# Eight tiles of P in the ring of attention, and low-half P V products one block later

## The chip, the cores and the metric

The kernel runs on one core of one Trainium2 chip. The metric is the device time of one execution in microseconds. Three runs of the kernel before took 2016.7, 2019.44 and 2020.83 us, so the median is 2019.44 us. The core has five engines that run their own instruction queues in order and wait for each other by semaphores: TensorE (PE in the profile, with weight loads apart as PEld), VectorE (DVE), ScalarE (ACT), GpSimd (POOL) and SyncE (SP, which here issues DMAs).

## The reference

A block of a transformer with adaptive layer norms: multi-head attention, then a token-shifting mixer and an MLP. What the change touches is the attention, and at its end the tiles of the tails. Cut to that:

```python
B, S, D, H = 1, 2048, 512, 32          # 32 heads of 16
mod = (_silu(c) @ w_mod).reshape(c.shape[0], 6, 1, -1)   # sa, ca, ga, sb, cb, gb
h = _layernorm(x) * (1 + ca) + sa
q, k, v = split(h @ wqkv)
scores = jnp.einsum("bhqd,bhkd->bhqk", q, k) * (Dh ** -0.5)
p = _softmax(scores, axis=-1)
o = jnp.einsum("bhqk,bhkd->bhqd", p, v)
x = x + ga * (o @ wo)
h = _layernorm(x) * (1 + cb) + sb
x = x + gb * _B_ref(h, w1, w2, w3, w4)  # layernorm, gelu, shifts by 1 and 2 tokens, MLP
```

All inputs are float32. The kernel keeps that precision by splitting operands into a high and a low half and adding up the products.

## The kernel before, in words

Attention is cut into 64 **units**. A unit is one quarter of the queries (512 of 2048) for one pair of heads, and has 16 **steps**, one for each 128 keys. There are 1024 steps, 256 for each quarter of the queries. A quarter of the queries is followed by a **tail** (output projection, second layer norm, mixer, MLP); three of the tails run after attention, and the first one starts 30 steps before its end.

For a step s and each of its two heads j the engines do this:

- PE computes scores into one PSUM bank (`sc`, L1012), ACT takes their exponential into the tile `pt[s]` (`pt<-sc`, L1008). `pt[s]` holds 2 x 512 words of 32 bits; the upper 16 bits of a word are read as float16, the high half of P.
- PE also computes the scores of step s+24 into another bank (`mb`, L996), and DVE reduces them to their maximum (`mx`, L992), which is needed when that unit begins. Four bank fills a step, two for ACT and two for DVE, share 7 PSUM banks (`NSM`).
- `p_low` (L1050) turns the lower 16 bits of `pt[s]` in place into a float16 number, the low half of P: one instruction of 128x1024 on POOL (L1061), or the same on ACT (L156 in the profile, a helper's line). The planner takes ACT when POOL's planned start is over 200 ns behind ACT's.
- PE multiplies V with P into the unit's own bank `pv`: four products of the high half for each step (L1086), and four of the low half for each pair of steps (L1083). "High product" and "low product" below mean such a group of four.

When a unit's last products are in, ACT copies `pv` to SBUF (`ac`, L1103), and only then may the first high product of the next unit start, as there is one `pv` bank. PE then transposes `ac` in four products (`ot`, L1113; eight records in the trace), ACT copies them (`sm`, L1120), DVE takes a reciprocal (`rc`, L1128), and POOL scales the result (`osb`, L1124). A unit's maxima are finished by one instruction on DVE (`mf`, L1042), two on ACT (`mf`, `nm`, L1043 and L1044) and one on POOL (`nm`, L1045).

The order of each engine's instructions is written out by the program. A planner (`Sched`) keeps one estimated clock for each engine. The loop at L1621 walks over **blocks** of three half steps (a half step is one head of one step). In each block it puts on PE a **row** (three `sc` and three `mb`), then the low halves that are due (on POOL or ACT), and then a **column**, the high and low products of what was computed two blocks earlier (`LAG`). Before a block, the planned clock of PE is set forward to when the banks of the row and the P of the column are ready, and if that leaves a gap of 500 ns, waiting work, such as `ot`, is put there. So the planned times decide which engine gets a low half and where `ot` and other small work stands; how long anything takes on the chip they don't decide.

The ring of P has six tiles (`NPT`). A tile comes free when PE has done the low product that reads it. A pair's low product stands two blocks behind its scores, and the next scores into the same tile come later on PE than it.

`fa` is a pool of SBUF that is opened after the first quarter of attention, when what held the weights of Q, K and V is closed. It holds the tiles of the tails, among them `xb` (4 of 128x512, float32) and `xn` and `xf` (3 each). The tails use them only from the last 30 steps on.

Of the kernel before, what the change touches and what calls it, by code (L numbers as in the profile page):

```python
# [8 lines left out]
F32 = mybir.dt.float32  # L9
# [3 lines left out]
I32 = mybir.dt.int32  # L13
# [7 lines left out]
S, D, H, DH, F = 2048, 512, 32, 16, 1792  # L21
P = 128
KT = D // P
NKT = S // P
CH = 512
# [58 lines left out]
XBF = 4  # L84
XBT = 4
# [7 lines left out]
XN = {"xn": 3, "xf": 3, "x4": 2}  # L93
# [5 lines left out]
NPT = 6  # L99
# [6 lines left out]
LNG = (1, 3)  # L106
LNC = 2
VP = 2
XB = 4


# [219 lines left out]
def kernel(ctx, tc, A_x, A_wqkv, A_wo, B_w1, B_w2, B_w3, B_w4, c, w_mod, out):  # L331
# [58 lines left out]
    for j in range(2):  # L390
        x = [ident[:, 64 * j + VD * a:64 * j + VD * a + DH + 1] for a in range(3)]
# [343 lines left out]
    for i in range(NV):  # L735
        t = qp.tile([P, H // 4, 192], BF16, name=f"vt{i}")
# [234 lines left out]
        sch.dma(dma.dma_start, vst[u], Vs[units[u][1]])  # L971

    sm = Slots(NSM)
    e_exp, e_hi, e_low, v_free, acs = {}, {}, {}, [0.0], []

    def bank(nm):
# [3 lines left out]
    def max_part(m, j):  # L980
# [14 lines left out]
                max_fin(u)  # L995
        return ready, lambda: te.matmul(b, lhs, kst[u % 3][r, c * CH:(c + 1) * CH], start=True, stop=True), after  # L996

    def score_part(s, j):

        u, kt = divmod(s, NKT)  # L1000
        if j == 0:
            pt[s] = at.tile([P, 2, CH], I32, name="pt", tag="pt", bufs=NPT)
        x, b = bank("sc")
        ready, sm.t[x] = sm.t[x], LATE
        r = slice(64 * j, 64 * j + 64)

        def after(e):
            ea = sch.crit("A", 480, e + PX, lambda: act.activation(pt[s][:, j], b, AF.Exp))  # L1008
            sm.t[x] = ea + XP["A"]
            if j:  # L1010
                e_exp[s] = e_hi[s] = ea
        return ready, lambda: te.matmul(b, kst[u % 3][r, kt * P:(kt + 1) * P], qst[u][r], start=True, stop=True), after  # L1012
# [210 lines left out]
    def pool_of(ci):  # L1223
        return fa if ci < NB or (ci - NB) % 2 else tp
# [58 lines left out]
    def tail(ci):  # L1283
# [91 lines left out]
        def normed(key, t, rs):  # L1375
            tag = xtag(key, t)
            xlive[tag] = xlive.get(tag, 0) + 1
            x = xn[key, t] = (tp if tag == "x4" else fa).tile([P, D], F32, name="xn", tag=tag, bufs=XN[tag])
            y = xbt[t]
            return ln_apply(x, y, rs), mark((key, t))  # L1380

# [15 lines left out]
        for i, t in enumerate(new):  # L1397
# [2 lines left out]
            yield from wo_mm(i, range(KT))  # L1400
            b = banks.pop(i)
            x1 = x1t[t]
            xb = xbt[t] = pool_of(ci).tile([P, D], F32, name="xb", tag="xb", bufs=XBF if pool_of(ci) is fa else XBT)

            def x1_add(x1=x1, b=b):
                dve.tensor_tensor(x1, x1, b, op=OP.add)
# [190 lines left out]


    blocks = [list(range(i, min(i + GRP, 2 * NS))) for i in range(-2 * LEAD, 2 * NS, GRP)]
    pvs = [x for s in range(0, NS, 2) for x in ((s, 0), (s + 1, 0), (s, 1))]  # L1600
    due = 0.0
    for k, blk in enumerate(blocks + [[]] * (LAG + CPER)):
        if blk and blk[0] <= LENDS <= blk[-1]:
# [69 lines left out]
        if blk and blk[0] <= 2 * (NS - T0L) <= blk[-1]:  # L1673
            sch.add(tail_loads())
# [56 lines left out]
```

## Time and profile before

| | us |
|---|---|
| median of the runs | 2019.44 |
| span of the profiled execution | 2019.7 |
| start, projections and the first quarter of attention, up to about step 264 | 550 |
| steps after the first quarter, looked at from 575 to 1480 | 905 |
| end of attention with the start of the first tail, 1480 to 1540 | 60 |
| tails, 1540 to the end | 480 |

The profile is of one execution. Its span, from the first instruction to the last, is 2019.7 us, which lies within the three runs, 0.3 us above their median; no time of its own is given for what lies around the span. The views used below are: busy time by stretch of time; groups of instructions, with the idle time of their engine ahead of them; who waited for whom; and the order of time of one engine, where neighbours of one kind are merged into one row (`x6` is six of them, the number behind the start is from the first's start to the last's end, and square brackets give idle time ahead and who ended it). Starts are counted from the span's start.

### The profile page before, as it was taken

Reading aid. Unit: us, or ns where it says so; the run is one execution under the profiler, and the core shown is the slowest. Engines: PE = TensorE matmul, PEld = TensorE weight load, DVE = VectorE, ACT = ScalarE, POOL = GpSimd, SP = SyncE. Lnnn points to the kernel's source line nnn. Section 1 sums busy time; section 2 is a strip of 40 time slices with the busy share of each in tenths; the row PEclk is TensorE's granted clock in tenths of the full one; section 3 lists DMA queues with packets and bytes.
Section 4 is the critical chain, followed back from the end, with each engine's and each line's share of the span. In section 5 each row is a group of like instructions: output and inputs, shape, how many; then the busy total and the mean of one; then the engine's idle time right before and its main releaser. Section 6 shows DMA issues by size and latency. Waiting matters only on the chain.

```text
span 2019.7 us, 41655 instructions
## 1 busy us (share of the span) xinstructions
PE 1934.4 (96%) x14456; PEld 1162.1 (58%) x14456; DVE 1656.3 (82%) x2979; ACT 1510.2 (75%) x3085; POOL 1571.9 (78%) x1488
## 2 busy tenths in 40 slices
PE   7999999999999999999999999999998999999999
PEld 5755545454444444444444444444455878898998
DVE  6398888879999999999999999999975886556443
ACT  6438987768999999999999999999985544344443
POOL 6349988879999999999999999999996554435222
PEclk9989999999999999999999999999999999999999
DMA  8777675445343434444443435354414676553541
GB/s 295 233 204 192 151 187 155 135 130 124 86 92 87 91 88 83 96 82 97 81 98 75 104 72 107 72 136 126 99 46 158 230 261 265 226 200 116 201 153 68
DMA packets 185508, 278.01 MB, mean 138 GB/s; under 512 B 117104, under 2 KB 127856, under 8 KB 169008
## 3 DMA queue, kind: packets, MB, share of 16 engines
q1 hardware_dynamic: 181792, 267.20, 49.1%
q10 hardware_dynamic: 2304, 4.20, 0.6%
q0 software_dynamic: 1200, 3.93, 0.5%
q8 instruction: 115, 1.88, 0.4%
q14 instruction: 97, 0.79, 0.1%
HBM read 211.81 MB, written 62.91 MB: 136 GB/s over the span
## 4 chain that ended last, share of the span: by engine, by line
PE 61%; DVE 16%; ACT 9%; issue 6%; POOL 4%; DMA 3%; SPq 0%; ACTq 0%; POOLq 0%; DVEq 0%
PE mb L996 13%; DVE mx L992 12%; PE pv L1086 9%; PE sc L1012 8%; ACT pt L1008 7%; PE w L363 5%; PE w L359 5%; PE w L361 5%; PE pv L1083 4%; PE ot L1113 3%; POOL pt L1061 2%; PE xT L1247 1%; POOL trs L1356 1%; PE v L359 1%; DMA wr<-Ws 1%
## 5 line engine op out<-in xcount | busy, mean ns | idle before, releaser
L1061 POOL TENSOR_SCALAR pt<-pt 128x1024 f16<-128x1024 uint16 x953 | 1248.3, 1367 | 79.9 <-ACT pt L1008 76.7
L992 DVE TENSOR_REDUCE mx<-mb 128x1 f32<-128x512 f32 x2048 | 1250.0, 681 | 72.7 <-PE mb L996 63.5
L1008 ACT ACTIVATE pt<-sc 128x512 int32<-128x512 f32 x2048 | 1060.9, 614 | 123.5 <-PE mb L996 97.1
L996 PE MATMUL mb<-kst,qtl 62*128 62x512 f32 x2048 | 781.1, 461 | 20.5 <-ACT pt L1008 10.0
L1012 PE MATMUL sc<-qtl,kst 64*128 64x512 f32 x2048 | 739.3, 449 | 4.6 <-DVE mx L992 1.8
L996 PEld LDWEIGHTS mb<-kst,qtl 62*128 62x128 f32 x2048 | 358.9, 193 | 233.7 <-ACT pt L1008 160.4
L1012 PEld LDWEIGHTS sc<-qtl,kst 64*128 64x128 f32 x2048 | 336.6, 185 | 185.4 <-DVE mx L992 118.7
L1086 PE MATMUL pv<-pt,vst 128*32 128x512 f16 x4096 | 384.8, 397 | 20.6 <-ACT ac L1103 20.6
L1460 POOL TENSOR_TENSOR g<-sq,g 128x256 fp32r<-128x256 f32 (+1 forms) x124 | 96.8, 785 | 188.9 <-ACT g L1459 176.6
L1083 PE MATMUL pv<-pt,vst 128*32 128x512 f16 (+1 forms) x2048 | 220.8, 389 | 2.5 <-POOL pt L1061 2.4
L1086 PEld LDWEIGHTS <-vst 128*32 128x32 bf16 x4096 | 91.8, 93 | 227.2 <-issue 208.8
L361 PE MATMUL w<-A,wr 128*128 128x256 f32 (+1 forms) x520 | 153.4, 295 | 0.3 <-DVE A L349 0.3
L359 PE MATMUL w<-A,wr 128*128 128x256 f32 (+1 forms) x520 | 153.2, 295 | 0.3 <-ACT A L353 0.3
L363 PE MATMUL w<-A,wr 128*128 128x256 f32 (+1 forms) x520 | 153.1, 294 | 0.0
L1456 ACT ACTIVATE sq<-w 128x256 f32<-128x256 f32 (+1 forms) x130 | 52.1, 401 | 127.0 <-PE w L363 117.5
L363 PE MATMUL w<-wr,g 128*128 128x512 f32 x270 | 106.5, 394 | 3.1 <-POOL g L1460 3.1
L359 PE MATMUL w<-wr,g 128*128 128x512 f32 x270 | 106.9, 396 | 1.8 <-DMA wr<-Ws 1.8
L361 PE MATMUL w<-wr,g 128*128 128x512 f32 x270 | 106.1, 393 | 0.0
L1438 DVE SCALAR_TENSOR_TENSOR sq<-sq,w 128x256 f32<-128x256 f32 (+1 forms) x130 | 58.1, 449 | 56.5 <-ACT sq L1458 56.3
L359 PEld LDWEIGHTS w<-A,wr 128*128 128x128 f32 x520 | 98.7, 190 | 1.7 <-ACT A L353 0.5
L361 PEld LDWEIGHTS w<-A,wr 128*128 128x128 f32 x520 | 98.7, 190 | 1.6 <-DVE A L349 0.5
L363 PEld LDWEIGHTS w<-A,wr 128*128 128x128 f32 x520 | 98.6, 190 | 0.5 <-issue 0.5
(156 smaller groups left out, 2131.6 us busy)
## 6 DMA issues: line engine op xcount, KB each, us to landing
wr<-Ws SPq DMA_DIRECT2D x66, 1024.0 KB, 5.2
vst<-Vs SPq DMA_DIRECT2D x64, 768.0 KB, 5.7
kst<-Ks SPq DMA_DIRECT2D x126, 384.0 KB, 6.1
Ws<-wr SPq DMA_DIRECT2D x14, 1024.0 KB, 5.0
qtl<-Qs SPq DMA_DIRECT2D x128, 96.0 KB, 4.3
Vs<-vt SPq DMA_DIRECT2D x32, 384.0 KB, 4.2
Ks<-qk SPq DMA_DIRECT2D x16, 512.0 KB, 3.8
Qs<-qk SPq DMA_DIRECT2D x16, 512.0 KB, 3.0
```

The source lines that it names most:

```text
L359: te.matmul(o, lh, rh, start=first, stop=False)
L361: te.matmul(o, lh, rl, start=False, stop=False)
L363: te.matmul(o, ll, rh, start=False, stop=last)
L992: end = sch.crit("D", 605, e + PX, lambda: dve.reduce_max(mxs[u][:, j, g, c:c + 1], b, axis=AX.X))
L996: return ready, lambda: te.matmul(b, lhs, kst[u % 3][r, c * CH:(c + 1) * CH], start=True, stop=True), after
L1008: ea = sch.crit("A", 480, e + PX, lambda: act.activation(pt[s][:, j], b, AF.Exp))
L1012: return ready, lambda: te.matmul(b, kst[u % 3][r, kt * P:(kt + 1) * P], qst[u][r], start=True, stop=True), after
L1061: e_low[s] = XP["G"] + sch.crit("G", 1345, ready, lambda: pool.tensor_scalar(o, i, 0.5, 1.0, op0=OP.mult, op1=OP.mult))
L1083: te.matmul(acc[r:r + n, :], v[:, kt + i, c:c + n].bitcast(F16), pt[s + i].bitcast(F16)[:, j, 0::2], start=False, stop=kt == NKT - 2, skip ...
L1086: te.matmul(acc[r:r + 32, :], v[:, kt, r:r + 32], pt[s].bitcast(F16)[:, j, 1::2], start=kt == 0, stop=False, skip_group_check=True)
L1113: te.matmul(b[:, t * n:(t + 1) * n], ac[:, t * P:(t + 1) * P], smat.rearrange("p j d -> p (j d)"), start=True, stop=True)
L1460: ("G", cG(n), lambda: pool.tensor_tensor(lo, sq, hi, op=OP.subtract)), (None, 0, end), bank=b)
```

## The change

After the first 264 steps, and up to step 983, the ring of P has eight tiles: the six of before, and two that lie over the four `xb` tiles of the tails. For that the tiles `xb`, `xn` and `xf` of the pool `fa` become slices of three larger tiles, of the same sizes and taken in the same turn as before. In the same steps a low product is due three half steps later, which is one block; near a unit's end less, and the last pair of a unit has no delay.

```diff
+WIDE = range(S // CH * 64 + 8, 984)
+LOWLAG = 3
...
+    ptx = []
...
+    def new_pt(s):
+        if s in WIDE:
+            i = pn[0] % (NPT + len(ptx)) - NPT
+            pn[0] += 1
+            if i >= 0:
+                pt[s] = ptx[i]
+                return
+        pt[s] = at.tile([P, 2, CH], I32, name="pt", tag="pt", bufs=NPT)
...
-            pt[s] = at.tile([P, 2, CH], I32, name="pt", tag="pt", bufs=NPT)
+            new_pt(s)
...
+                x = xns[tag][:, xnum[tag] % XN[tag]]
...
-            xb = xbt[t] = pool_of(ci).tile([P, D], F32, name="xb", tag="xb", bufs=XBF if pool_of(ci) is fa else XBT)
+            xb = xbt[t] = xbs[:, t % XBF] if pool_of(ci) is fa else tp.tile([P, D], F32, name="xb", tag="xb", bufs=XBT)
...
-    pvs = [x for s in range(0, NS, 2) for x in ((s, 0), (s + 1, 0), (s, 1))]
+    pvs = []
+    for s in range(0, NS, 2):
+        low = 2 * s + 2 + (min(LOWLAG, 2 * (NKT - 2 - s % NKT)) if s in WIDE else 0)
+        pvs += [(2 * s, s, 0), (2 * s + 2, s + 1, 0), (low, s, 1)]
+    pvs.sort(key=lambda x: x[0])
...
-            while pvs and 2 * (pvs[0][0] + pvs[0][1]) < x and not (col and pvs[0][0] % NKT == 0 and not pvs[0][1]):
-                col.append(pvs.pop(0))
+            while pvs and pvs[0][0] < x and not (col and pvs[0][1] % NKT == 0 and not pvs[0][2]):
+                col.append(pvs.pop(0)[1:])
...
+            xbs = fa.tile([P, XBF, D], F32, name="xbs")
+            xns = {k: fa.tile([P, XN[k], D], F32, name=k) for k in ("xn", "xf")}
+            xnum = {"xn": 0, "xf": 0}
+            ptx += [xbs[:, 2 * i:2 * i + 2].bitcast(I32) for i in range(2)]
```

No instruction is added or removed, but as the planner's times move, so does the order. Of the 1024 low halves, 953 stand on POOL and 71 on ACT before; with the change 938 and 86. Fourteen of those fifteen are moved within the steps 264 to 983, where ACT has 60 before and 74 now. In both the order repeats every 48 steps, which is three units and happens 15 times: four low halves on ACT before, five now.

The first place is **ACT around the copy `ac`** in the middle of the stretch. The rows are `pt<-sc` for exponentials (of one head each), `pt<-pt` for a low half, and `ac`, `sm`, `mf` and `nm` as above. Before:

```order
L1008 ACTIVATE pt<-sc 128x512 x21
L156 ACTIVATE pt<-pt 128x1024
L1103 ACTIVATE ac<-pv 128x512
L1008 ACTIVATE pt<-sc 128x512 x6
L1120 ACTIVATE sm<-ot 128x136
```

With the change (two tiles of the ring now go by the name `xbs`):

```order
L1022 ACTIVATE pt<-sc 128x512 x8
L1117 ACTIVATE ac<-pv 128x512
L1022 ACTIVATE pt<-sc 128x512 x3
L158 ACTIVATE pt<-pt 128x1024
L1022 ACTIVATE pt<-sc 128x512
L1022 ACTIVATE xbs<-sc 128x512 x4
L1022 ACTIVATE pt<-sc 128x512 x2
L1057 ACTIVATE mf<-mf 128x8
```

Before, a low half stands directly ahead of `ac` in 15 of these 45 units. With the change it does so in none; in 14 it stands three exponentials behind `ac`. The others stand, by three units: ahead of `sm` (twice), between `sm` and `mf`, and six exponentials ahead of `ac`.

The second place is **PE around the transposes `ot`**, in the middle of the stretch too. L1086 (now L1100) is a high product, L1083 (now L1097) a low one, `sc` and `mb` are the row that follows. Before:

```order
L1086 LDWEIGHTS vst
L1086 MATMUL pv<-pt,vst 32x512
L1113 MATMUL ot<-smat,ac 128x34 x4
L996 MATMUL mb<-kst_967,qtl_965 128x512
L1012 MATMUL sc<-qtl_145,kst_147 128x512 x2
```

With the change:

```order
L1097 LDWEIGHTS vst
L1097 MATMUL pv<-xbs,vst 32x512
L1127 MATMUL ot<-smat,ac 128x34 x4
L999 MATMUL mb<-kst_147,qtl_145 128x512
L1026 MATMUL sc<-qtl_965,kst_967 128x512 x2
```

Before, the column ahead of `ot` is one high product in 37 of the units in the stretch. With the change it is a high and a low product in 27 units and one high product in 15, and in two of three units `ot` stands six to nine steps later in its unit. Ahead of the tails, DVE, SP and POOL change the place of small work by a few rows; in the tails themselves the order is as before.

More of the change, by code (lines that the diff above doesn't have):

```diff
@@ L996, in max_part @@
         return ready, lambda: te.matmul(b, lhs, kst[u % 3][r, c * CH:(c + 1) * CH], start=True, stop=True), after
+    pn = [0]
+    def new_pt(s):
[6 more added lines that the diff above has]
+        pt[s] = at.tile([P, 2, CH], I32, name="pt", tag="pt", bufs=NPT)
     def score_part(s, j):
@@ L1377, in normed @@
             xlive[tag] = xlive.get(tag, 0) + 1
-            x = xn[key, t] = (tp if tag == "x4" else fa).tile([P, D], F32, name="xn", tag=tag, bufs=XN[tag])
+            if tag == "x4":
+                x = tp.tile([P, D], F32, name="xn", tag=tag, bufs=XN[tag])
+            else:
+                x = xns[tag][:, xnum[tag] % XN[tag]]
+                xnum[tag] += 1
+            xn[key, t] = x
             y = xbt[t]
```

## The prediction

> **What bounds the kernel now.** I read the page first for the span and the chain that ended last, then the busy time by stretch.
>
> ```profile
> span 2019.7 us, 41655 instructions
> PE 61%; DVE 16%; ACT 9%; issue 6%; POOL 4%; DMA 3%; SPq 0%; ACTq 0%; POOLq 0%; DVEq 0%
> 575.00:1480.00 905.00, 876.12 (x7457) 414.53 (x7457) 868.27 (x1510) 837.37 (x1657) 867.75 (x739) 1.00 0.44 93
> ```
>
> The change acts on steps 264 to 983, of which the third row shows nearly all: 905 us, then the busy time of PE, weight loads, DVE, ACT and POOL. The granted clock is 1.00, so no clock is to be won. DVE (868.27) and POOL (867.75) are both busy for 96% of it, ACT for 93%. PE shows 876.12, but the ends of its matmuls are modelled and a wait inside a group of products counts as busy. So the 61% of PE in the chain is no proof that PE sets the pace, and I look at who waits, in the same stretch:
>
> ```profile
> L992 DVE TENSOR_REDUCE mx<-mb 128x1 f32<-128x512 f32 x1422 | 864.5, 681 | 30.9 <-PE mb L996 24.7 <-PE sc L1012 3.1
> L1061 POOL TENSOR_SCALAR pt<-pt 128x1024 f16<-128x1024 uint16 x651 | 847.5, 1363 | 31.9 <-ACT pt L1008 29.4
> L156 ACT ACTIVATE pt<-pt 128x1024 f16<-128x1024 uint16 x60 | 82.5, 1375 | 0.0
> PEld mb L996 <- ACT pt L1008: 130.2, 381, 0.8
> PE pv L1086 <- ACT ac L1103: 17.5, 15, 1.2
> PEld L1083 <- issue: 15.9, 36, 0.5
> ACT pt L1008 <- POOL pt L1061: 0.8, 2, 0.4
> ```
>
> Maxima follow each other on DVE with almost no gap: 864.5 us for 1422 of them is 0.608 us each, and a step has two. What is left for DVE to win is its idle time, 905 - 868 = 37 us, and 24.7 of that is a wait for PE to fill a bank. PE in its turn is held by ACT, which has not emptied a bank (130.2 us in 381 waits of the weight loads, mostly hidden), and by two waits that this change can move: 17.5 us in 15 waits of the first high product of a unit for `ac`, and 36 pauses in low products, 15.9 us.
>
> The order repeats every three units, and so does the time:
>
> ```profile
> 621.62:641.76 20.14, 20.00 (x176) 9.43 (x174) 19.88 (x36) 18.41 (x39) 20.02 (x18) 1.00 0.44 89
> 641.76:661.65 19.89, 19.29 (x170) 8.92 (x167) 19.13 (x34) 18.41 (x38) 19.53 (x17) 1.00 0.38 80
> 661.65:682.63 20.98, 19.65 (x166) 9.39 (x165) 19.67 (x35) 19.76 (x39) 19.04 (x18) 1.00 0.48 98
> ```
>
> The third unit of the three takes 0.8 to 1.1 us more than the others. DVE is idle in it for 1.3 us (20.98 - 19.67), in the first for 0.3. 45 units at 61.0 / 3 make 915 us for the steps of the change.
>
> **The long unit, term 1.** In order of time, such a unit shows the following (ACT's rows, PE's with the bracket on `ac`, then DVE's):
>
> ```profile
> 1032.95 1.35 ACT L156 ACTIVATE pt<-pt 128x1024 f16<-128x1024 uint16 x1
> 1034.14 0.60 ACT L1103 ACTIVATE ac<-pv 128x512 f32<-128x512 f32 x1
> 1034.79 0.64 PE L1086 MATMUL pv<-pt,vst 128*32 128x512 f16 x8 [1.16 <-ACT ac L1103]
> 1031.76 3.67 DVE L992 TENSOR_REDUCE mx<-mb 128x1 f32<-128x512 f32 x6
> 1036.16 1.89 DVE L992 TENSOR_REDUCE mx<-mb 128x1 f32<-128x512 f32 x3 [0.73 <-PE mb L996]
> ```
>
> A low half runs on ACT directly ahead of `ac`; it holds ACT for 1.19 us (1034.14 - 1032.95). PE stands for 1.16 us, the next row comes late, and DVE runs dry for 0.73 us. This is the place that the order of ACT in the section on the change shows, and with the change no low half stands directly ahead of `ac`. It happens 15 times, so the term is 15 x 0.73 = **-11.0 us**. Its ends are 0, if something else is late next, and -17.5, all of PE's wait. What is late next is the transposes `ot` a column later, which are term 4.
>
> **The pauses in low products, term 2.** The rows of another unit, the second of the three:
>
> ```profile
> 1015.27 0.40 PE L1083 MATMUL pv<-pt,vst 128*32 128x512 f16 x4
> 1018.95 0.77 PE L1083 MATMUL pv<-pt,vst 128*32 128x512 f16 x4
> 1022.78 0.50 PE L996 MATMUL mb<-kst,qtl 62*128 62x512 f32 x1 [0.47 <-ACT pt L1008]
> 1017.87 1.40 ACT L156 ACTIVATE pt<-pt 128x1024 f16<-128x1024 uint16 x1
> 1024.57 1.29 DVE L992 TENSOR_REDUCE mx<-mb 128x1 f32<-128x512 f32 x2 [0.56 <-PE mb L996]
> ```
>
> A low product normally takes 0.40 us. The one at 1018.95 takes 0.77, because its second tile is just then being made on ACT (1017.87 to 1019.27). One block later, about 1.9 us by 1.5 steps of 20.3 / 16 us, that half is long done, so the pauses go. What they are worth is less clear. DVE did not run dry for five microseconds after this one; at 1024.57 it did, for 0.56, after PE had also waited 0.47 us for ACT. After most of the 36 pauses DVE goes on without a gap. Ends: 0 (other engines cover it) and -15.9 us (the row above). I take 15 x 0.37 (0.77 - 0.40), only the pauses of this kind of unit, and three quarters of that, since the wait for ACT behind it stays: **-4 us**.
>
> **Low halves from POOL to ACT, term 3.** Fourteen more within the stretch. ACT gets 14 x 1.19 = 17 us more, of 905 - 837 = 68 us that it has idle; POOL gets 14 x 847.5 / 651 = 18 us less. ACT's own time is thus covered on average, but while a low half runs, the banks of `sc` behind it come free 1.2 us late, and behind it on ACT stand exponentials, for whose banks PE waits in order, and behind them the rows that feed DVE. That cover is there at most places:
>
> ```profile
> 635.63 1.38 ACT L156 ACTIVATE pt<-pt 128x1024 f16<-128x1024 uint16 x1
> 634.26 7.38 DVE L992 TENSOR_REDUCE mx<-mb 128x1 f32<-128x512 f32 x12
> 1045.25 1.39 ACT L156 ACTIVATE pt<-pt 128x1024 f16<-128x1024 uint16 x1
> 1040.61 9.65 DVE L992 TENSOR_REDUCE mx<-mb 128x1 f32<-128x512 f32 x16
> ```
>
> Here twelve maxima, and sixteen, run on through a low half on ACT. So of the three kinds of low halves on ACT that don't stand at `ac`, one is followed by the gap of 0.56 us and two by none. By that a low half costs 0 to 0.73 us (the row at `ac`), and 0.56 / 3 = 0.19 on average: 14 x 0.19 = **+2.5 us**, with ends 0 and 10. The lighter POOL is worth nothing by the rows: in 905 us one engine waited for it directly, ACT, 0.8 us in two waits.
>
> **The transposes, term 4.**
>
> ```profile
> 1012.78 0.41 PE L1086 MATMUL pv<-pt,vst 128*32 128x512 f16 x4
> 1013.12 1.08 PE L1113 MATMUL ot<-smat,ac 128*128 128x34 f32 x8
> 1014.67 1.89 DVE L992 TENSOR_REDUCE mx<-mb 128x1 f32<-128x512 f32 x3 [0.21 <-PE mb L996]
> 1038.59 1.89 DVE L992 TENSOR_REDUCE mx<-mb 128x1 f32<-128x512 f32 x3 [0.54 <-PE mb L996]
> ```
>
> `ot` holds PE for 1.0 us between two rows, and DVE runs dry behind it, for 0.21 us in the second of the three units and for 0.54 in the long one, where the wait for `ac` has just emptied its banks. Without that wait the long unit's should be like the other's: 15 x 0.33 = -5 us. But in 27 units a low product now stands ahead of `ot` besides the high one, and a second product takes PE 0.24 us more (0.64 for two, 0.40 for one, in the rows above): 27 x 0.24 = +6.5 if each is felt, 0 if `ot`, which now stands elsewhere in the unit, finds DVE with full banks. I take +5, nearer to the end where it is felt, since both units above are dry there: together **0**, with ends -5 and +6.5.
>
> **What costs nothing.** The ring itself: in 905 us ACT waited for a tile of the ring as little as the 0.8 us of its row; PE's own order covers it, since the low product that frees a tile stands on PE ahead of the scores that refill it. With a low product one block later that tile would come free a block too late in a ring of six; eight tiles give that block back. The tiles that lie over `xb` are used by the tails only after step 983, so nothing waits there. Slices of one tile in place of tiles by themselves have the same sizes and turns. In the tails the order is unchanged, so their 480 us only shift. Price of all this 0, with ends -0.8 and +2 for the seam at step 984, of which the trace has no row of its own.
>
> The Trainium skill, Perfetto Trace Analysis, section Identifying Performance Opportunities, says that a gap that repeats on the engine that should be saturated can mean too few buffers. DVE's repeating 30.9 us is such a gap; by that rule two more tiles could be worth up to that, by the row of 0.8 us they are worth nothing alone. It stands below as a rival.
>
> **The sum.** -11.0 - 4 + 2.5 + 0 = -12.5 us, on the profiled 2019.7: **2007.2 us**. The median of the runs, 2019.44, is 0.3 lower than that span, which I leave out.
>
> **The rivals.**
>
> - *POOL was the bound.* Then what counts is its share: 14 halves x 1.30 us = -18 us, 2001.5 us, in place of the terms above. For it: POOL is as busy as DVE (867.75 and 868.27). Against it: nobody waits for POOL but for 0.8 us, and POOL's own 29.4 us of idle time are waits for ACT. Chance 0.16. The Trainium skill (same page and section) names the engine with the highest occupancy as the one to relieve; by that rule POOL ties with DVE, and the rows of waits break the tie.
> - *The repeating bubble closes whole.* With the two waits of PE gone, DVE would never run dry: -30.9 us, 1988.8 us. For it: PE's two waits together are 33 us. Against it: `ot` still stands between two rows. Chance 0.06.
> - *The wait moves.* The `ac` wait goes, but `ot`, now behind two products and with `sm` directly behind a low half on ACT, takes what was won: terms 1 and 4 at -11 and +6.5, term 3 at half its end, +5, and nothing for the pauses: 2020.2 us, between 2016 and 2023. For it: DVE runs dry at `ot` with one product already. Against it: two of three `ot` stand where no `ac` has just held PE. Chance 0.18.
> - *Slower: ACT's low halves starve DVE.* Each of the 14 added ones costs what the one ahead of `ac` costs now, 0.73 us of DVE: +10.2, with `ot` at +6.5 and term 1 at -11.0, and nothing for the pauses: +5.7, 2025.4 us. It decides from 0.32 us for each added half ((11.0 - 6.5) / 14), if the pauses are worth nothing. For it: the 0.56 us behind one of the three kinds. Against it: DVE's rows of twelve and of sixteen. Chance 0.13.
>
> That the change doesn't do what it says can be left out: the order shows the eight tiles and the late products.
>
> **How the numbers follow.** My forecast of 2007.2 (2003 to 2015.4) has 0.47. Within 0.2% of before, which is about what a measurement of this kernel can tell from no change, means 2015.4 to 2023.5. Faster: 0.47 + 0.16 + 0.06 = 0.69. Same: 0.18. Slower: 0.13. The range of 8 in 10 takes in POOL as the bound and the wait that moves, and leaves out the closed bubble and most of the slower case: from 1997.5 us (the POOL case with the pauses' 4 us besides) to 2023 us.
>
> **What would show it.** In the stretch up to about step 984, the wait of the first high product for `ac` falls from 17.5 us to near 0 (term 1); the pauses ahead of low products in the weight loads fall from 36 to few (term 2); ACT's low halves rise from 60 to 74 and DVE's idle time falls by about 12 us in the same number of steps (term 3); DVE's gap behind `ot` is 0.2 to 0.45 us in every unit (term 4). Attention ends about 12 us earlier, and what follows it takes as long as before. I am wrong if DVE's idle time does not fall though `ac` is not waited for, or if POOL's idle time grows by less than it was relieved while the steps get shorter, which would make POOL the bound, or if the tails change.

## The result, and the profile after

| | before | with the change |
|---|---|---|
| median of the runs, us | 2018.09 (four runs, 2016.70 to 2020.83) | 2004.03 (four runs, 2000.79 to 2006.74) |
| profiled execution: own time | – | 2006.74 |
| profiled execution: span | 2019.7 | 2004.8 |
| end of the last low product of attention | 1533.7 | 1513.7 |
| from there to the end | 486 | 491.1 |

The ratio of the runs is 0.9927, with a 95% interval of 0.9911 to 0.9943: **14 us, 0.7%, faster**. The same code was measured again beside the first experiments, where it took 1999.7 us against 2020.33, a ratio of 0.9898 (0.9883 to 0.9913).

The page with the change, first its span and then the chain that ended last:

```profile
span 2004.8 us, 41627 instructions
PE 61%; DVE 11%; DMA 4%; ACT 4%; POOL 3%; issue 2%; SPq 1%; ACTq 0%; POOLq 0%; DVEq 0%
```

PE's 61% of the chain did not move by a point, while 15 us went. As the prediction said, that share does not show what sets the pace. The shares of DVE and ACT, 16% and 9% before, are 11% and 4% now.

Busy time by stretch: first the stretch that answers to the one shown of before, then three units that answer to its three (us, then busy time of PE, weight loads, DVE, ACT and POOL, the granted clock, the DMA share and GB/s):

```profile
575.00:1465.00 890.00, 878.79 (x7461) 409.62 (x7465) 868.22 (x1511) 847.26 (x1675) 851.30 (x727) 1.00 0.45 94
618.97:638.86 19.89, 19.89 (x174) 9.28 (x173) 19.59 (x35) 19.23 (x39) 19.07 (x17) 1.00 0.42 86
638.86:658.82 19.96, 19.43 (x174) 8.90 (x171) 19.29 (x36) 18.57 (x38) 19.43 (x18) 1.00 0.40 83
658.82:678.90 20.08, 19.98 (x162) 9.28 (x162) 19.74 (x35) 19.39 (x40) 19.00 (x18) 1.00 0.49 100
```

DVE's busy time is the same 868.2 us, now in 890 us where it was in 905, so its idle time fell from 36.7 to 21.8 us. POOL has 16 us less to do, ACT 10 us more. The long unit of 20.98 us is gone. Groups of instructions in 575 to 1465 (count, busy time, mean ns; then idle time ahead and who ended it):

```profile
L995 DVE TENSOR_REDUCE mx<-mb 128x1 f32<-128x512 f32 x1422 | 864.7, 678 | 19.5 <-PE mb L999 14.5 <-PE sc L1026 3.9
L158 ACT ACTIVATE pt<-pt 128x1024 f16<-128x1024 uint16 x58 | 81.2, 1400 | 0.0
L158 ACT ACTIVATE xbs<-xbs 128x1024 f16<-128x1024 uint16 x15 | 20.7, 1379 | 0.0
```

The window holds the same 1422 maxima as the one of before, so the comparison is clean: 864.5 us of work then and 864.7 now, 30.9 us of idle time then and 19.5 now. Who waited for whom in that stretch (total us, times, longest):

```profile
PEld mb L999 <- ACT pt L1022: 107.5, 297, 0.8
PEld L1097 <- issue: 24.9, 103, 0.3
ACT pt L1022 <- POOL xbs L1075: 4.0, 13, 0.3
DVE mx L995 <- PE mb L999: 14.5, 36, 3.3
PE mb L999 <- DMA kst<-Ks: 3.5, 1, 3.5
```

The row "PE pv <- ACT ac" with its 17.5 us is not there any more. The row of low products is still there and larger, 103 times in place of 36, which is a trap: it is a different wait. At most 0.3 us, on average 24.9 / 103 = 0.24 us, is the ordinary hold of the weight loads of a product that stands first in its column. Before, a low product always stood behind a high one and had no such hold; its 36 rows were of up to 0.5 us and were real pauses. What tells the two apart is the product itself, since a pause stretches it. Counted so from the trace (over 80 ns between two of the four starts), the low products of steps 264 to 983 had 36 pauses of 11.3 us in total before and have none now.

The place of term 1, in order of time: PE, then ACT, then DVE.

```profile
1040.39 0.41 PE L1100 MATMUL pv<-xbs,vst 128*32 128x512 f16 x4
1040.63 0.40 PE L1097 MATMUL pv<-xbs,vst 128*32 128x512 f16 x4
1041.95 0.64 PE L1100 MATMUL pv<-pt,vst 128*32 128x512 f16 x8
1041.22 0.64 ACT L1117 ACTIVATE ac<-pv 128x512 f32<-128x512 f32 x1
1043.13 1.46 ACT L158 ACTIVATE pt<-pt 128x1024 f16<-128x1024 uint16 x1
1034.85 12.59 DVE L995 TENSOR_REDUCE mx<-mb 128x1 f32<-128x512 f32 x21
```

`ac` starts 0.59 us after the unit's last low product does (1041.22 - 1040.63), the next unit's first high products carry no bracket, the low half runs 1.9 us behind the start of `ac`, and 21 maxima go on through all of it. Before, DVE ran dry here for 0.73 us.

The last row of the waits is new. Before, no engine waited for a DMA in this stretch; with the change PE stands once, in step 920, for a load of keys (`kst`), until 1368.61. SyncE sent that load at 1358.73, after a wait of 3.5 us of its own for a load of the tails' weights (`wr`), whose place in SyncE's order had moved. DVE runs dry there for 3.35 and 1.21 us, and the granted clock is 0.50 from 1367.9 to 1374.7. The 48 steps from 912 on take 65.3 us, where the twelve times 48 steps from step 288 to 863 take 59.7 each. So some 5.5 us of what the change wins are lost at this one place.

Two more things were not foreseen. Attention ended 20 us earlier, and what follows it took 5 us longer.

### The profile page after: what moved, and what is told of

Same layout as the page of the kernel before. It is cut to its first block, busy times and chain, and to the rows that moved or that the text cites. A ratio compares the mean times of both kernels' runs of the same rounds, so it can differ in the third digit from the quotient of the medians.

```text
span 2004.8 us, 41627 instructions
## 1 busy us (share of the span) xinstructions
PE 1939.3 (97%) x14456; PEld 1161.6 (58%) x14456; DVE 1656.6 (83%) x2979; ACT 1519.9 (76%) x3100; POOL 1551.9 (77%) x1473
## 4 chain that ended last, share of the span: by engine, by line
PE 61%; DVE 11%; DMA 4%; ACT 4%; POOL 3%; issue 2%; SPq 1%; ACTq 0%; POOLq 0%; DVEq 0%
PE mb L999 15%; PE sc L1026 10%; PE pv L1100 10%; DVE mx L995 8%; PE w L365 5%; PE w L361 5%; PE w L363 5%; PE pv L1097 4%; PE ot L1127 3%; ACT pt L1022 2%; DMA wr<-Ws 2%; POOL pt L1075 1%; PE xT L1261 1%; POOL trs L1370 1%; PE q L365 1%
## 5 line engine op out<-in xcount | busy, mean ns | idle before, releaser
L1075 POOL TENSOR_SCALAR pt<-pt 128x1024 f16<-128x1024 uint16 x773 | 1017.7, 1367 | 73.0 <-ACT pt L1022 72.6
L1022 ACT ACTIVATE pt<-sc 128x512 int32<-128x512 f32 x1688 | 890.3, 623 | 94.7 <-PE mb L999 65.6
L1100 PE MATMUL pv<-pt,vst 128*32 128x512 f16 x3376 | 318.6, 396 | 4.6 <-ACT ac L1117 4.6
L1479 POOL TENSOR_TENSOR g<-sq,g 128x256 fp32r<-128x256 f32 (+1 forms) x124 | 96.7, 784 | 189.7 <-ACT g L1478 176.0
L1075 POOL TENSOR_SCALAR xbs<-xbs 128x1024 f16<-128x1024 uint16 x165 | 219.6, 1363 | 4.4 <-ACT xbs L1022 4.3
L1022 ACT ACTIVATE xbs<-sc 128x512 int32<-128x512 f32 x360 | 200.0, 639 | 10.9 <-PE mb L999 9.5
L1100 PEld LDWEIGHTS <-vst 128*32 128x32 bf16 x4096 | 91.4, 94 | 182.9 <-issue 164.5
L1097 PE MATMUL pv<-pt,vst 128*32 128x512 f16 (+1 forms) x1688 | 173.0, 392 | 1.3 <-POOL pt L1075 1.3
L361 PE MATMUL w<-wr,g 128*128 128x512 f32 x270 | 108.6, 402 | 3.0 <-DMA wr<-Ws 3.0
L365 PE MATMUL w<-wr,g 128*128 128x512 f32 x270 | 108.0, 400 | 3.1 <-POOL g L1479 3.1
L363 PE MATMUL w<-wr,g 128*128 128x512 f32 x270 | 107.7, 399 | 0.0
L363 PEld LDWEIGHTS w<-A,wr 128*128 128x128 f32 x520 | 99.6, 191 | 1.7 <-DVE A L351 0.5
```

The source lines that it names most:

```text
L361: te.matmul(o, lh, rh, start=first, stop=False)
L363: te.matmul(o, lh, rl, start=False, stop=False)
L365: te.matmul(o, ll, rh, start=False, stop=last)
L1075: e_low[s] = XP["G"] + sch.crit("G", 1345, ready, lambda: pool.tensor_scalar(o, i, 0.5, 1.0, op0=OP.mult, op1=OP.mult))
L1097: te.matmul(acc[r:r + n, :], v[:, kt + i, c:c + n].bitcast(F16), pt[s + i].bitcast(F16)[:, j, 0::2], start=False, stop=kt == NKT - 2, skip ...
L1100: te.matmul(acc[r:r + 32, :], v[:, kt, r:r + 32], pt[s].bitcast(F16)[:, j, 1::2], start=kt == 0, stop=False, skip_group_check=True)
```

## The experiments

All of them are read in the same way. *Stretch* is the time from the first exponential of step 264 to that of step 984, in the profiled execution; *`ac` waits*, *pauses* and DVE's gaps are counted in it from the trace. *48 steps* is the mean time of three units over the steps 288 to 863; it leaves out the wait in step 920, which is in every kernel with the change's order of SyncE (2.0 to 3.5 us) and not in `before`, `ring_only` and `lag_only`. Fifteen times 48 steps make the stretch. Two executions of the changed code gave 900.6 and 900.2 us, and two of the kernel before's order (with and without the wider ring) 917.6 and 917.1, so a difference of 1.5 us is near what one profile can tell.

| kernel | low products | low halves on ACT | `ac` waits, us | pauses, us | stretch, us | 48 steps, us | ratio to before (95%) |
|---|---|---|---|---|---|---|---|
| before | at once | 60 | 15, 17.5 | 36, 11.3 | 917.6 | 61.13 | 1 |
| ring_only | at once | 60 | 15, 17.5 | 40, 11.9 | 917.1 | 61.09 | 1.0003 (0.9989 to 1.0017) |
| before_moved | at once | 60 | 0 | 56, 27.3 | 924.7 | 61.31 | 1.0049 (1.0034 to 1.0064) |
| before_pool | at once | 45 | 0 | 76, 31.1 | 917.3 | 61.04 | 1.0022 (1.0009 to 1.0034) |
| replan_only | at once | 74 | 0 | 58, 14.9 | 910.7 | 60.52 | 0.9954 (0.9938 to 0.9969) |
| lag_only | a block later | 60 | 15, 14.8 | 0 | 909.0 | 60.55 | 0.9957 (0.9943 to 0.9972) |
| after_atac | a block later | 74 | 14, 15.2 | 0 | 909.4 | 60.35 | 0.996 (0.9945 to 0.9976) |
| after_pool | a block later | 60 | 0 | 6, 3.7 | 907.5 | 60.25 | 0.9947 (0.9931 to 0.9964) |
| the change, after_again | a block later | 74 | 0 | 0 | 900.2 | 59.69 | 0.9898 (0.9883 to 0.9913) |
| after_89 | a block later | 89 | 0 | 0 | 906.7 | 60.13 | 0.9933 (0.9916 to 0.9949) |
| after_89_b | a block later | 89 | 15, 6.9 | 0 | 910.1 | 60.57 | 0.9961 (0.9946 to 0.9976) |

### The three parts of the change, each alone

The ring of eight tiles, with the low products at once:

```diff
-LOWLAG = 3
+LOWLAG = 0
```

> Eight tiles in the ring, but no low product later: every engine's order is that of the kernel before, only the tiles differ. My theory (the ring is worth nothing by itself, since PE's own order frees a tile before it is refilled): last low product starts at 1533 us, give or take 2, and the whole time is within 0.2% of before. If the ring of six was what the engines waited for: last low product near 1514 us, as in the changed kernel.

Measured: 2020.02 us, and a stretch of 917.1 us with the same 15 waits for `ac`. The ring alone is worth nothing, as the prediction had it.

Two kernels split the rest. The planner takes the due times from one list, and PE's products are put out by another:

```diff
-    pvs.sort(key=lambda x: x[0])
+    planned, pvs = order_of(0), order_of(LOWLAG)
...
-        for s, i in col:
+        for s, i in plan:
             start = max(start, pv_ready(s, i) - t)
```

In `lag_only`, as shown here, ACT, DVE, POOL and SyncE keep the order of before, and only PE's low products come a block later. In `replan_only` the two lists are exchanged: those four engines have the order of the change, and the low products are due at once.

> Low products one block later on PE, with eight tiles, but planned as before, so that ACT, DVE, POOL and SP keep the order of the kernel before to the last row. My theory: the pauses in low products (36, 11 us) go, and the 15 waits of a unit's first high product for the copy of the unit before stay at 17 us; the last low product starts at 1533 - 4 = 1529 us (1522 to 1534). Rival, the place of the low products itself is the gain: near 1514 us, as in the changed kernel.

> The order of ACT, DVE, POOL and SP of the changed kernel to the last row, with 74 low halves on ACT in the stretch, but the low products on PE where they stood before. My theory: the waits for the copy go (0 in place of 15), pauses in low products stay (36 or more, and a few longer ones); the last low product starts at 1533 - 14 = 1519 us (1515 to 1524). POOL as the bound: 1514 us, since all of POOL's relief is in it. The lag as the only gain: 1533 us.

> The changed kernel once more. In its profile attention ended 20 us earlier than before, but the rest took 5 us longer, at a granted clock of 0.93 and 0.97 in stretches where it was 1.00 before. If the clock there is a matter of the execution: the last low product again at 1513 us, and the rest between 486 and 491 us, with the clock of the stretch behind attention telling which. If the change itself makes the rest longer: 491 us at any clock.

Measured: 2012.83, 2011.87 and 1999.7 us. The stretches give what each part is worth: the later products 8.1 us (917.1 to 909.0) with the old order and 10.3 us (910.7 to 900.4, the mean of two) with the new one; the new order 6.4 us without the later products (917.1 to 910.7) and 8.6 us with them (909.0 to 900.4). Singly they make 14.5 us, together 17. The new order carries the wait in step 920, though. By the 48 steps, taken 15 times, the later products are worth 8.1 us with the old order and 12.5 with the new one, the new order 8.6 and 12.9, and both 21: they help each other by some 4 us. Not run were later products in a ring of six tiles; that they need the two added tiles is argued in the prediction and not shown.

In `lag_only` the waits for `ac` are still there:

```profile
PE pv L1100 <- ACT ac L1116: 14.8, 15, 1.0
DVE mx L995 <- PE mb L999: 18.0, 40, 1.0
POOL pt L1075 <- POOL nm L1059: 0.2, 1, 0.2
```

PE stands almost as long for `ac` as before, 14.8 us against 17.5. The gaps that DVE has right behind those waits, counted from the trace, fall from 8.9 to 3.4 us, but the gaps two steps later, behind `ot`, rise from 6.8 to 12.0, so almost nothing is won there. What is won stands at another place. The gap of 0.56 us that the prediction shows at 1024.57, some five microseconds behind a pause, comes back every 48 steps and makes 6.7 us before; with the later products 0.7 us of it are left. That is 6 of the 7.9 us by which DVE's idle time falls from `before` to `lag_only`. In `replan_only`, `before_moved` and `before_pool`, which have the pause ahead of it, the gap makes 6.2 to 6.5 us.

### Is the wait for `ac` enough by itself?

In the kernel before, the 15 low halves directly ahead of `ac` were put elsewhere: three steps earlier on ACT (`before_moved`), or on POOL (`before_pool`). The planner's rule is replaced by a list of steps. As its times change with that, it also puts `ot` elsewhere in ten of the 45 units, and a load of the tails' weights elsewhere in SyncE's order:

```diff
-        if g > a + LACT:
+        if s in ON_ACT:
```

> The kernel before, with one edit: in 15 units the low half that stood on ACT directly ahead of the copy is taken from a step three earlier, so that six exponentials stand between it and the copy; POOL and ACT keep their shares (60 on ACT in the stretch). My theory (term 1): the 15 waits of 1.16 us are gone and the last low product starts at 1533 - 11 = 1522 us (1517 to 1527). POOL as the bound: no change, 1533 us, since no share moves.

> The kernel before, with those 15 low halves on POOL instead: 45 on ACT in the stretch, POOL gets 15 x 1.30 = 20 us more. My theory (DVE is the bound, POOL is covered): the waits for the copy are gone all the same, last low product at 1533 - 11 = 1522 us, or 1 to 3 us less as ACT has less to do. POOL as the bound: 1533 + 20 = 1553 us.

Measured: 2028.24 and 2023.03 us, 0.5% and 0.2% slower than before, and in both no wait for `ac` is left. Some 5 of the 7.1 us by which the stretch of `before_moved` grew stand in the steps 864 to 911, where PE waits once for keys (2.3 us); the stretch of `before_pool` did not grow, so what it lost stands outside of it. By the 48 steps both are about as long as before. So taking the waits away won nothing by itself. The wait has moved. One low product of `before_moved` in order of time on PE:

```profile
1038.96 0.39 PE L1085 MATMUL pv<-pt,vst 128*32 128x512 f16 x1
1039.83 0.41 PE L1085 MATMUL pv<-pt,vst 128*32 128x512 f16 x3 [0.47 <-POOL pt L1063]
```

The first row is the first of its four products; the other three stand for 0.47 us until POOL has made the low half that they read. Such pauses rise to 56 with 27.3 us and, in `before_pool`, to 76 with 31.1 us. In these two, where low products are due at once and POOL is not relieved, the low half that is taken from the place at `ac` makes another low half late for its product. `replan_only`, which takes the waits away and relieves POOL, has 58 pauses with 14.9 us, and gains. Even there the pauses eat a part, which is one reason why the two parts of the change are worth more together.

### With the later products: the place at `ac`, and POOL's share

In the changed kernel, the 14 low halves that stand three exponentials behind `ac` were put back directly ahead of it (`after_atac`, ACT's load unchanged), or given to POOL (`after_pool`, ACT's load as before), by the same edit with other lists.

> The changed kernel, with the low half on ACT that stands three exponentials behind the copy, in 14 units, taken from a step two earlier, so that it stands directly ahead of the copy again; shares as in the changed kernel, products a block later. My theory: 14 waits of about 1.1 us come back, last low product at 1513 + 14 x 0.73 = 1523 us (1519 to 1530). If shares or the lag make the gain: 1513 us.

> The changed kernel, with those 14 low halves on POOL: 60 on ACT in the stretch, as before the change. My theory: ACT's extra share cost a little, last low product at 1513 - 2.5 = 1511 us (1503 to 1514). POOL as the bound: 1513 + 18 = 1531 us.

Measured: 2010.85 and 2008.45 us. The 14 waits for `ac` cost 9.0 us (909.4 against 900.4), near the prediction's 14 x 0.73 = 10. That part held in size. But 14 low halves on POOL, without any wait for `ac`, cost 7.1 us (907.5 against 900.4), where the prediction had a small gain. Busy time by stretch of `after_pool`:

```profile
575.00:1465.00 890.00, 875.92 (x7414) 409.52 (x7412) 861.95 (x1500) 827.45 (x1647) 860.60 (x736) 1.00 0.44 94
```

POOL, the last of the five, is busy for 860.60 of 890 us, 96.7%, and ACT for 827.45. Where that hurts shows at the end of a unit (PE, ACT, DVE, in order of time):

```profile
1060.44 0.39 PE L1099 MATMUL pv<-xbs,vst 128*32 128x512 f16 x1
1061.06 0.40 PE L1099 MATMUL pv<-xbs,vst 128*32 128x512 f16 x3 [0.24 <-POOL xbs L1077]
1061.50 0.60 ACT L1119 ACTIVATE ac<-pv 128x512 f32<-128x512 f32 x1 [0.51 <-PE pv L1099]
1061.96 1.89 DVE L997 TENSOR_REDUCE mx<-mb 128x1 f32<-128x512 f32 x3 [0.52 <-PE mb L1001]
```

The unit's last low product is torn in two, because POOL is late with the last low half; `ac` waits 0.51 us for it; and DVE runs dry for 0.52 us. That product is the one which the change does not delay ("the last pair of a unit has no delay"; by the formula in the diff it is the only pair with less than three half steps). The same place with the change:

```profile
1059.96 0.40 PE L1097 MATMUL pv<-xbs,vst 128*32 128x512 f16 x4
1060.40 0.60 ACT L1117 ACTIVATE ac<-pv 128x512 f32<-128x512 f32 x1
1057.22 5.52 DVE L995 TENSOR_REDUCE mx<-mb 128x1 f32<-128x512 f32 x9
```

Four products together, `ac` 0.44 us behind, no gap among nine maxima. In the trace of `after_pool` the low halves on POOL at steps 41 and 42 of every 48 begin 2.8 us behind their exponentials (median), with the change 1.6 to 1.8 us. But the last low product is torn in only 6 of the 15 groups of 48 steps, and each time the steps behind it come some 0.6 us later than with the change. DVE's gap of about 0.5 us is there in 13 of the 15 groups. In seven of these 13 the product is whole and `ac` no later than with the change; in all seven the planner, with other times, had put the `ot` ahead of it three half steps earlier, and some 0.7 us are lost in that unit. So about half of the price is POOL's lateness, by the trace. The other half stands where `ot` has moved too, and this kernel does not tell the two apart.

So the two are worth more together as well. From `lag_only` (15 waits for `ac`, 60 on ACT), by the 48 steps taken 15 times, taking the waits away with POOL's load as it was gains 4.5 us (`after_pool`), relieving POOL with the waits as they were gains 3.0 us (`after_atac`), and both together gain 12.9. By the stretches it is 1.5 us, nothing and 8.6; but these three kernels have a wait for a DMA at about step 920, which `lag_only` has not. The Trainium skill, Perfetto Trace Analysis, section Identifying Performance Opportunities, calls the engine with the highest occupancy the one to optimize first. By that rule DVE and POOL tied here, and for POOL the measurement agrees in part: the relief was worth 3.0 us with the waits for `ac` in place, and at most 8.4 us with them gone (`after_pool` against the change, with what stands at `ot`).

### Is a still lighter POOL better?

Fifteen more low halves on ACT, at steps 20 (`after_more`) or 21 (`after_more_b`) of every 48:

> The changed kernel with 15 more low halves on ACT (89 in the stretch, six in three units), none of them directly ahead of the copy; the added one stands behind the transposes' copies or behind six exponentials of a unit. If POOL, at 97% busy with 60 low halves on ACT and 96% with 74, still sets the pace together with DVE: attention's last low product 5 to 7 us earlier than the changed kernel's 1511 to 1513 us, near 1506. If DVE alone is the bound by now (868 of 890 us busy): no change, 1511 to 1514. If the added low halves starve DVE, as my prediction priced them, 0.19 to 0.73 us each: 1515 to 1524 us.

> The same share, 89 low halves on ACT, but the added one of three units taken one step later, which makes the planner put it closer to the transposes and the maxima's small work. If only the share counts: as in after_more, within 1 us. If the place of a low half among ACT's other work counts as much: apart from it by 3 us or more.

Measured: 2161.4 and 2166.64 us, ratios 1.0688 (1.067 to 1.0706) and 1.0726 (1.0699 to 1.0753), stretches of 1060.5 and 1063.8 us. That is not ACT's 18 us. Who waited, in `after_more` from 700 to 1300:

```profile
PE sc L1028 <- DMA qtl<-nm: 82.1, 9, 9.4
SPq L139 <- PE mb L1001: 83.5, 13, 13.5
```

PE stands nine times for up to 9.4 us, once every three units, for the rows that bring a unit's maxima (`nm`) into the tile of queries, `qtl`. POOL's and SyncE's rows around one of these:

```profile
1059.44 0.20 POOL L1061 TENSOR_TENSOR nm<-mf,nm 128x8 fp32r<-128x8 f32 x1
```

```profile
1065.39 0.30 SPq L139 DMA_DIRECT2D qtl<-Qs  x1
1065.75 0.41 SPq L139 DMA_DIRECT2D kst<-Ks  x1
1066.26 0.37 SPq L139 DMA_DIRECT2D qtl<-Qs  x1
1066.68 0.41 SPq L139 DMA_DIRECT2D kst<-Ks  x1
1067.18 7.63 SPq L139 DMA_DIRECT2D qtl<-nm  x8
```

`nm` is ready at 1059.64, but in SyncE's queue four loads stand ahead of its eight rows, and these wait until PE is done with the buffers. They leave at 1065.39; the eight rows leave from 1067.18 to 1074.81, and PE's scores start at 1075.23. The added low half had changed the planned times, and they the order of SyncE. In the whole stretch there are 14 such waits, 120.8 us. So this pair says nothing about ACT's load.

Two more kernels put the fifteen where the orders of PE, DVE and SyncE stay those of the change: at step 9 of every 48, in the middle of a unit, and at step 46.

> The changed kernel with 15 more low halves of P on ACT (89 in steps 264 to 983), at steps 9 of every 48, in the middle of a unit, where the orders of PE, DVE and SyncE stay word for word those of the changed kernel (in the two kernels with 89 before they did not). If ACT's load made those two slow, this one is slow as well: above 2100 us. If the place of the shift rows in SyncE's order did, PE no longer waits for qtl<-nm, and the stretch is near the changed kernel's 900 us: 893 to 897 if POOL, now 20 us lighter, still held it; 900 to 905 if POOL no longer matters and PE (98.7% busy) does; 908 or more if a fifteenth low half on ACT costs DVE the 0.56 us of the rows of before each (15 x 0.56 = 8.4).

> The same with the 15 more low halves at steps 46 of every 48, six exponentials behind sm in the last third of the third unit; orders of PE, DVE and SyncE as in the changed kernel. If the place within a unit matters little, the stretch agrees with the kernel beside it within 2 us. If a low half on ACT near the end of a unit makes the copy ac late, waits of the first high product for ac come back (up to 15 x 1 us) and the stretch is 908 us or more.

Measured: 2005.89 and 2011.90 us. The 150 us are gone. The 120.8 us of them that are waits for `nm` came from SyncE's order; the orders of PE and DVE went back with it, so the rest is not told apart. But both are slower than the change: in `after_89`, with neither a wait for `ac` nor a pause, the stretch grew by 6.3 us, 0.42 for each added half, and DVE's idle time rose from 21.6 to 26.3 us, none of the rise behind `ot` or `ac`. In `after_89_b` the waits for `ac` came back as well, 15 with 6.9 us. So 74 low halves on ACT lie between two sides that both lose: fourteen fewer cost 7 us, about half of it through POOL, and fifteen more cost 6 and 10 us at the two places tried. No kernel tried was faster than the change.

### What follows attention

The 5 us after attention lie in its first stretches. Busy time by stretch, first before, behind a pause of PE in the tails, then with the change:

```profile
1605.00:1612.40 7.40, 7.02 (x54) 6.76 (x55) 6.49 (x12) 5.83 (x16) 6.19 (x6) 1.00 0.74 243
```

```profile
1585.00:1592.40 7.40, 7.40 (x44) 6.82 (x45) 6.36 (x12) 5.76 (x15) 6.13 (x6) 0.77 0.78 260
1600.00:1607.30 7.30, 6.93 (x24) 5.63 (x25) 2.77 (x6) 0.82 (x1) 0.93 (x3) 0.77 0.59 245
1637.00:1644.30 7.30, 7.30 (x33) 6.22 (x32) 7.11 (x14) 6.02 (x12) 6.97 (x10) 0.77 0.39 139
1692.00:1699.30 7.30, 7.30 (x51) 7.30 (x50) 4.24 (x9) 5.14 (x13) 1.91 (x3) 0.77 0.01 2
```

The granted clock is 1.00 in the first row and 0.77 in the four of the change, 7.3 us each, so 4 x 7.3 x 0.23 = 6.7 us of PE's clock are missing there. In each of the four it is 0.50 for 3.4 us and 1.00 for the rest. The second profiled execution of the change has the cut at four like places and the same 491 us behind attention. The pauses of PE ahead of such places, first with the change, then before:

```profile
1584.98 0.98 PE L1261 MATMUL xT<-ident,xf 128*128 128x128 f32 x7 [2.14 <-ACT xf L1381]
1600.37 0.80 PE L361 MATMUL w<-wr,g 128*128 128x512 f32 x1 [2.35 <-DMA wr<-Ws]
```

```profile
1605.38 0.98 PE L1247 MATMUL xT<-ident,xn 128*128 128x128 f32 x7 [2.52 <-ACT xn L1367]
```

A pause of 2.52 us left the clock whole, and one of 2.14 us was followed by the cut. The pause is not new, then, and its length alone does not decide. Nor does every execution of the change seem to lose as much: the four runs of the first measurement have mean clocks of 0.988, 0.988, 0.991 and 0.991 and take 2006.74, 2006.54, 2001.51 and 2000.79 us. The Trainium skill, TensorE: Matmul & The Clock Gate, says in its Part 1 that the activity window of 3.4 us runs freely, so that the same kernel fares differently from run to run; the four runs agree with that. Its table under "Why this matters for your kernels" advises against pauses above some 3 us; here one of 2.1 us was followed by a cut, and the measurement decides. Whether the shorter attention makes the cut more likely stays open: the four runs of the second measurement, at clocks of 0.989 and 0.991 to 0.992, took 2003.63 and 1999.1 to 1999.9 us.

## Why the prediction was right, and where its terms were not

**The direction and the total.** 2007.2 us were forecast, and 2004.03 measured, well inside the range. The forecast's whole saving was 12.5 us; the stretch shortened by 17, and the runs by 14 in one measurement and 20.6 in the other, as the clock behind attention allowed.

**What bounds the kernel.** The reading that DVE's idle time is what can be won, that PE's busy share is no bound, and that two waits of PE hold DVE, was right: DVE's busy time stayed at 868.2 us and all 15 us of its stretch came out of idle time.

**Term 1, the waits for `ac`, -11.0 us.** Right in place and near in size: 9.0 us for 14 of them, or 9.9 by the 48 steps (`after_atac`). The working left out a condition: they are worth this where the low products come later and POOL is relieved. With the low products at once and POOL not relieved, taking the waits away won nothing (`before_moved`, `before_pool`); with later products and POOL's load as it was, it gained 1.5 us by the stretch and 4.5 by the 48 steps.

**Term 2, the pauses in low products, -4 us.** Right in kind, mis-sized by a factor of two: the later products alone measured -8.1 us, and -10.3 with the new order. The step that failed is "three quarters of that, since the wait for ACT behind it stays", on a price of 0.37 us, which is PE's pause. The wait for ACT did stay, 15 times with 6.9 us before and 4.7 us in `lag_only`, but DVE's gap behind it went, 6.7 us before and 0.7 then. By DVE's 0.56 us, which stands in the rows shown, the term would have been 15 x 0.56 = 8.4 us. The upper end in the range, -15.9, did hold it.

**Term 3, 14 more low halves on ACT, +2.5 us.** Wrong in sign as measured: -7.1 us (the change against `after_pool`). The step that failed is "the lighter POOL is worth nothing by the rows". The rows of before show who waited while another wait stood in front of POOL's; with that one gone, POOL's late low halves become the next thing late, at the one low product of a unit that is not delayed. The trace shows this for about half of the 7.1 us; the cause of the other half, where `ot` moved too, stays open. ACT's own price was there, and larger than thought: 0.42 us for each further half (`after_89`), not 0.19, and inside its ends of 0 to 0.73.

**Term 4, the transposes, 0 us.** In the maxima it came out as forecast: their gaps behind `ot`, counted from the trace, make 12.0 us before and 12.3 with the change, in 45 units. What the term did not have is the reciprocal `rc`, which waits on DVE for `sm`: 6.3 us in five units before, 1.2 in two with the change. So all of DVE's gaps behind `ot` together fell by 4.8 us. Two gaps of maxima with the change:

```profile
1032.93 1.89 DVE L995 TENSOR_REDUCE mx<-mb 128x1 f32<-128x512 f32 x3 [0.23 <-PE mb L999]
1055.30 1.29 DVE L995 TENSOR_REDUCE mx<-mb 128x1 f32<-128x512 f32 x2 [0.56 <-PE mb L999]
```

Both stand behind an `ot` with both products in front (the columns start at 1030.82 and 1053.19). The first is about as long as the 0.21 us of before; the second is above the 0.45 us foretold. The mean, 12.3 / 45 = 0.27 us, lies within the 0.2 to 0.45 us foretold. What the second product costs, the total does not tell.

**Cost of nothing.** The ring alone measured 1.0003 (0.9989 to 1.0017). The order ahead of the tails was priced at nothing, and there the step failed: SyncE's moved load made PE wait for keys in step 920, which cost some 5.5 us. The tails' order did not change, but their time did in the profiled execution, by 5 us, and the granted clock is lower in it. Neither was foreseen.

**The rivals.** "POOL was the bound", at 2001.5 us, was half right: its mechanism is real, but little of it could be had alone, since relieving POOL with the waits for `ac` in place gains 3 us by the 48 steps and nothing by the stretch (`after_atac` against `lag_only`). "The wait moves" did not happen in the change, though it is what happens when only a part of it is done: to the low products in `before_moved`, in six units to POOL's last low half in `after_pool`. "ACT's low halves starve DVE" shows fifteen halves further on, at 0.42 us for each. The bubble did not close whole: 19.5 of 30.9 us are left, 4.6 of them at step 920.

**The signs named ahead.** The waits for `ac` gone, 60 to 74 low halves, idle time down by 14.9 us for some 12 foretold: these came. The count of rows ahead of low products did not fall but rose to 103, because the sign was badly chosen: the row mixes a pause with the ordinary hold. Two of the signs of being wrong came as well. POOL's idle time grew by 2 us only (37.3 to 39.2 in the stretch), less than the 19 us by which it was relieved (880.3 to 861.4 busy), while the steps got shorter, "which would make POOL the bound". The sign was too weak for that: `lag_only` shortened the stretch by 8.1 us with POOL's load as it was, which POOL as the bound does not allow. And the tails changed, by the 5 us above.

## What to carry to other kernels

When two engines are both busy for 96% of a stretch, and a third waits at one place, a wait of nearly zero in the rows of a profile says only that this engine is not late *yet*: price a relief also for the case that the wait in front of it is gone, and expect two fixes to be worth more together than singly (12.9 us against 4.5 and 3.0). A pause costs what the engine that sets the pace loses by it, which may show some microseconds later: price it by that engine's gap. When a planner's numbers move, compare the order of every queue, the DMA queue's too: a row of small transfers behind four loads cost over 120 us here and looked like a cost of the engine that had got the work, and one load that moved took back 5.5 us of the change itself.

## What the runs showed of the hardware that was not expected

A pause of PE of 2.14 us was followed by 7.3 us with a granted clock of 0.77 on average in one execution, while one of 2.52 us ahead of the same kind of transposes (`xT`) in another left it at 1.00. The 3.49 us for which PE waits for keys in step 920 came with 6.8 us at 0.50. With PE standing up to 9.4 us every three units (`after_more`), the granted clock of the stretch is 0.93:

```profile
575.00:1465.00 890.00, 772.09 (x6300) 352.63 (x6299) 736.64 (x1275) 729.11 (x1424) 705.84 (x600) 0.93 0.37 78
```

So a wait there costs PE twice: the time for which it stands, and slower matmuls behind it.
